# Sliding-window attention with a gated MLP: TensorE transposes the inputs of three batches instead of four, and the hand order of all engines is rewritten

## The chip, the cores and the metric

The kernel runs on one core of one Trainium2 chip, as one launch. The metric is the device time of that launch in microseconds (us), lower is better. Five engines work side by side, each through its own queue in order: TensorE (PE; its weight loads are shown as PEld), VectorE (DVE), ScalarE (ACT), GpSimd (POOL) and SyncE (SP), which here only issues DMA transfers.

## The reference

Causal attention with a window of 64 positions over 8 batches, 8 heads, 576 positions and head size 64; then a gated MLP with a spatial matrix. All inputs and the output are float32.

```python
scores = scale * np.matmul(q, k.transpose(0, 1, 3, 2))        # scale = 1/8
mask = (rel >= 0) & (rel < window)                            # window = 64
attn = softmax(np.where(mask, scores, -1e9))                  # 1e-9 is added to the sum
x = np.matmul(attn, v), heads side by side                    # (8, 576, 512)
h = np.maximum(x @ w_in, 0.0)                                 # 512 -> 1024
u, v = h[..., :512], h[..., 512:]
v_n = (v - mean(v)) / np.sqrt(var(v) + 1e-6)
v_s = np.einsum('ts,bsd->btd', w_spatial, v_n) + b_spatial[None, :, None]
return (u * v_s) @ w_out                                      # (8, 576, 512)
```

## The kernel before, in words

The whole program is one list of words, `ORDER`, that a loop at the end turns into instructions one after the other. There is no scheduler behind it: each word emits its instructions to the engine that it names, so the sequence of words is the sequence of every engine's queue. In a word the first number is the batch b. The second is mostly the pair of heads s (0 to 3, or 4 for the last 64 positions of all pairs) or the block of 128 positions or features j, m or r. A last letter A, D or P says which of ACT, DVE and POOL does a copy.

A batch goes through these steps:

- `l`, `lv`: SP issues the loads of q, k and v in float32. `wl` does it for the eight pieces of w_in; `wsp` and `wout` are issued by POOL.
- `c`, `cv`: casts of q and k, and of v, to float16 (L331 to L346). `sh` (L349 to L360) makes a second copy of v whose keys are shifted by 64 positions. `wc` (L254) casts a piece of w_in on the chip.
- q and k must have the head dimension on the partitions. There are two ways, chosen by `NPE` (L147). For b < NPE the words `T` (L378, L381) are TensorE transposes into a PSUM tile, four for each word, and `to` (L388, L391) copies that tile to SBUF on ACT or DVE: ten `T` and ten `to` a batch, with casts by pair of heads. From batch NPE on the word `R` (L369) is one VectorE transpose of 32x32 blocks of half of q or of k: four a batch, each of [128, 576] 32-bit words, with casts of half of q or k (1152 columns, L337). The loads of q and k differ too: ten a batch (eight of 256 KB and two of 128 KB) in the first way, sixteen of 144 KB, one for each head, in the second; v takes nine and five loads.
- `S`: the scores of two heads. In the first way (L410) 16 matmuls that contract over 64 rows; in the second (L421) 32 that contract over 32 rows, two of them accumulating into each output. `S.b.4` is the last block of queries for all pairs.
- `E` (L453, L460) exponentiates on ACT, `M` (L469) masks on DVE by a minimum with a table, `P` (L486, L496) multiplies by ones (for the sum) and by v on TensorE.
- `n1`, `n2` (L502, L509): logarithm and exp(-log) of the sum on ACT; `x` (L517): the product on DVE, which is x in float16.
- `V` and `Q` (L531, L543): the second half of x @ w_in, block of positions by block; `Q.b` also does the last block of the output of batch b-1 in the other half of the array. `vo` copies with a maximum, `bs` (L562) takes mean and variance, `rs` and `ln` (L580) normalise.
- `U` (L589, L594): the first half of x @ w_in, transposed; `ru` copies it. `G` (L612): the spatial matrix; `g` (L619): the product with `ru`. `O` (L626): the product with w_out; `oc` (L633) copies and `st` stores.
- `W` and `wo` transpose w_spatial once, in the first batch. `H.n` are n matmuls on zeros, at the start only.

Scores and the tile that `P` writes (for s < 4) share a ring of two PSUM tiles ("att", two banks each); all else that TensorE writes goes through a ring of four tiles of one bank ("mm"). A `P` or `S` therefore also waits until the tile two places before it in the ring has been read: a score tile by `E`, a tile of `P` by `x`.

The matmuls use the array in different shapes (rows by columns): 128x128 for `T`, `V`, `U`, `G`, `O`, `W` and `H`; 64x128 for `T.b.x.4`; 128x64 for `P` and `Q`; 64x64 for `S` in the first way; 32x64 for `S` in the second. The transposed scores of one `S` in the first way are written like this:

```python
for h in (0, 1):
    d = slice(64 * h, 64 * h + 64)
    nc.tensor.matmul(sc[r:r + 64, h, o0:o0 + c1 - c0],
                     K[d, p, 64 * key:64 * key + 64], Q[d, p, c0:c1],
                     start=True, stop=True)
```

Of the kernel before, what the change touches and what calls it, by code (L numbers as in the profile page):

```python
# [14 lines left out]
S = 576  # L15
# [17 lines left out]
V.0.0.3.4 vo.0.2.D l.1.q.2 wc.0.0.A V.0.1.0.1 l.1.k.2 bs.0.3 V.0.1.1.2 vo.0.0.A V.0.1.2.3 l.1.k.3
V.0.1.3.4 wc.0.2.A wc.0.1.P T.1.q.0 lv.1.2 vo.0.1.A Q.0 to.1.q.0.D c.1.k.0.P U.0.0 l.1.q.3 vo.0.4.A
cv.1.0.D U.0.4 bs.0.2 ru.0.0 T.1.k.0 U.0.3 sh.1.0.1.D to.1.k.0.A bs.0.4 c.1.q.1.P ones.0 S.1.0
ru.0.4 sh.1.0.0.D U.0.2 E.1.0 bs.0.0 l.1.k.4 U.0.1 bs.0.1 ru.0.3 ru.0.2 T.1.q.1 M.1.0 T.1.k.1 ru.0.1
W.1 to.1.q.1.D rs.0 lv.1.5 W.0 wo.1.A ln.0.4 P.1.0 ln.0.2 to.1.k.1.A c.1.q.2.P W.4 wo.0.D n1.1.0
lv.1.4 ln.0.1 S.1.1 W.2 ln.0.3 n2.1.0 ln.0.0 l.1.q.4 T.1.q.2 wo.4.A W.3 wo.2.D c.1.k.3.P E.1.1
wo.3.D G.0.1 lv.1.6 wout x.1.0 lv.1.7 ones.1 to.1.q.2.D c.1.k.2.P G.0.4 l.2.k.0 M.1.1 T.1.k.2 G.0.2
c.1.k.4.A g.0.1 lv.2.1 cv.1.1.A g.0.4 l.2.q.0 T.1.k.3 sh.1.1.0.P g.0.2 G.0.0 cv.1.2.A to.1.k.2.A  # L40
sh.1.1.1.P c.1.q.4.D c.1.q.3.A sh.1.2.1.P S.1.2 to.1.k.3.D P.1.1 lv.2.0 E.1.2 sh.1.2.0.D T.1.q.4
T.1.k.4 g.0.0 G.0.3 to.1.q.4.A n1.1.1 M.1.2 n2.1.1 lv.1.8 T.1.q.3 g.0.3 P.1.2 l.2.k.1 to.1.k.4.D
n1.1.2 O.0.2 x.1.1 l.2.q.1 n2.1.2 to.1.q.3.D O.0.0 cv.1.3.P l.2.k.2 oc.0.2.A x.1.2 sh.1.3.0.A S.1.3
c.2.k.0.D S.1.4 lv.2.5 E.1.3 O.0.3 oc.0.0.D sh.1.3.1.D lv.2.3 O.0.1 E.1.4 c.2.q.0.D oc.0.3.A M.1.3
l.2.q.4 T.2.q.0 T.2.k.0 oc.0.1.D to.2.q.0.A P.1.3 cv.1.4.D n1.1.3 V.1.1.0.2 M.1.4 sh.1.4.0.P lv.2.2
V.1.3.0.2 n2.1.3 to.2.k.0.D V.1.3.2.3 l.2.q.3 P.1.4 x.1.3 S.2.0 c.2.q.1.P n1.1.4 l.2.q.2 cv.2.0.D
V.1.1.2.3 n2.1.4 V.1.1.3.4 st.0.2 V.1.3.3.4 x.1.4 vo.1.1.A U.1.1 sh.2.0.0.P lv.2.8 vo.1.3.D E.2.0
c.2.k.1.P lv.2.6 bs.1.1 V.1.2.0.2 sh.2.0.1.P l.2.k.3 V.1.0.0.2 c.2.k.2.A M.2.0 T.2.k.1 ru.1.1
V.1.0.2.3 V.1.2.2.3 to.2.k.1.D V.1.2.3.4 lv.2.7 T.2.q.1 cv.2.1.P vo.1.2.A V.1.0.3.4 bs.1.3 st.0.1
P.2.0 vo.1.0.A sh.2.1.1.P Q.1 to.2.q.1.D n1.2.0 l.2.k.4 c.2.q.4.A bs.1.0 c.2.q.2.P S.2.1 vo.1.4.A  # L50
lv.2.4 T.2.k.2 sh.2.1.0.P bs.1.2 T.2.q.2 oc.0.4.A U.1.4 c.2.q.3.P to.2.q.2.A to.2.k.2.D U.1.2 ru.1.4
lv.3.0 n2.2.0 bs.1.4 U.1.3 E.2.1 lv.3.3 x.2.0 c.2.k.3.P U.1.0 rs.1 l.3.q.3 M.2.1 ru.1.2 l.3.k.2
T.2.q.4 ln.1.0 S.2.2 ru.1.3 st.0.0 ln.1.2 P.2.1 ru.1.0 to.2.q.4.D l.3.q.0 ln.1.4 T.2.q.3 n1.2.1
ln.1.1 lv.3.1 T.2.k.3 ln.1.3 G.1.0 E.2.2 to.2.q.3.D l.3.k.0 cv.2.3.A lv.3.6 G.1.1 M.2.2 n2.2.1
sh.2.3.1.P st.0.3 to.2.k.3.D cv.2.4.A G.1.3 x.2.1 cv.2.2.P l.3.q.1 sh.2.3.0.A c.2.k.4.D sh.2.2.1.A
sh.2.2.0.D S.2.3 g.1.0 lv.3.5 T.2.k.4 E.2.3 P.2.2 g.1.3 G.1.2 lv.3.2 n1.2.2 g.1.1 lv.3.4 n2.2.2
M.2.3 G.1.4 to.2.k.4.A l.3.q.2 x.2.2 P.2.3 g.1.2 l.3.k.3 n1.2.3 S.2.4 O.1.1 g.1.4 E.2.4 l.3.k.4
c.3.k.2.D n2.2.3 sh.2.4.0.D O.1.2 l.3.k.1 M.2.4 c.3.q.0.A x.2.3 V.2.2.0.4 oc.1.1.A oc.1.2.A T.3.q.0
c.3.k.0.A vo.2.2.D O.1.0 cv.3.1.P to.3.q.0.A bs.2.2 c.3.q.3.P cv.3.2.A P.2.4 T.3.k.0 n1.2.4 oc.1.0.D
V.2.1.0.4 sh.3.2.1.P n2.2.4 c.3.q.1.A st.1.0 x.2.4 V.2.0.0.4 vo.2.1.D sh.3.1.1.A cv.3.0.P l.4.q.1  # L60
lv.4.1 to.3.k.0.D O.1.3 sh.3.1.0.A c.3.k.1.P st.0.4 bs.2.1 vo.2.0.A sh.3.0.0.P V.2.3.0.4 l.3.q.4
oc.1.3.A bs.2.0 l.4.k.3 sh.3.0.1.P T.3.k.2 vo.2.3.A T.3.k.1 c.3.q.2.P T.3.q.1 l.4.k.4 to.3.k.1.A
S.3.0 to.3.q.1.D c.3.k.3.P l.4.q.3 Q.2 E.3.0 to.3.k.2.D sh.3.2.0.P l.4.q.0 l.4.q.2 S.3.1 vo.2.4.A
M.3.0 T.3.q.2 cv.4.1.P U.2.2 E.3.1 to.3.q.2.D lv.4.0 bs.2.4 T.3.k.3 oc.1.4.A c.3.q.4.P P.3.0 l.4.k.2
ru.2.2 to.3.k.3.D c.3.k.4.P S.3.2 n1.3.0 T.3.q.3 M.3.1 U.2.0 E.3.2 lv.3.8 bs.2.3 U.2.1 st.1.4 n2.3.0
M.3.2 to.3.q.3.A lv.4.3 U.2.3 x.3.0 ru.2.0 rs.2 T.3.q.4 T.3.k.4 ru.2.3 ln.2.2 P.3.2 ln.2.0 ru.2.1
P.3.1 ln.2.1 lv.4.2 to.3.q.4.A ln.2.4 n1.3.2 U.2.4 ln.2.3 G.2.3 n1.3.1 lv.3.7 n2.3.1 cv.3.4.D st.1.3
G.2.1 to.3.k.4.D ru.2.4 sh.3.4.0.P x.3.1 n2.3.2 l.4.q.5 cv.4.0.P st.1.2 x.3.2 G.2.0 st.1.1
sh.4.0.1.P g.2.1 l.4.k.1 S.3.4 g.2.0 l.4.q.7 S.3.3 c.4.q.0.P G.2.2 E.3.3 l.4.k.0 g.2.3 l.4.q.6
cv.3.3.P cv.4.2.A G.2.4 l.4.q.4 g.2.2 sh.3.3.1.P cv.4.3.A O.2.1 g.2.4 E.3.4 l.4.k.6 sh.3.3.0.P M.3.3  # L70
O.2.0 l.4.k.5 sh.4.1.0.P M.3.4 l.4.k.7 oc.2.1.A P.3.3 n1.3.3 O.2.2 l.5.q.1 sh.4.0.0.P R.4.q.0 n2.3.3
O.2.3 oc.2.2.A x.3.3 oc.2.0.A lv.5.2 V.3.0.0.4 c.4.k.0.D l.5.q.2 V.3.3.0.4 R.4.k.0 vo.3.0.A
c.4.q.1.P l.5.k.0 oc.2.3.D P.3.4 l.5.k.3 S.4.0 bs.3.0 n1.3.4 sh.4.1.1.P S.4.1 E.4.0 vo.3.3.D
V.3.2.0.4 lv.5.0 c.4.k.1.P R.4.q.1 n2.3.4 V.3.1.0.4 x.3.4 M.4.0 lv.5.4 U.3.0 vo.3.1.A R.4.k.1 E.4.1
Q.3 bs.3.3 vo.3.2.A P.4.0 lv.5.3 ru.3.0 bs.3.2 lv.4.4 S.4.2 oc.2.4.A bs.3.1 vo.3.4.A U.3.1 n1.4.0
bs.3.4 U.3.2 cv.5.0.P lv.5.1 n2.4.0 M.4.1 l.5.q.7 rs.3 U.3.3 l.5.q.0 E.4.2 x.4.0 U.3.4 l.5.q.3
ln.3.4 ru.3.1 ln.3.1 P.4.1 l.5.k.1 ln.3.0 n1.4.1 S.4.3 ln.3.3 l.5.k.2 ln.3.2 ru.3.2 G.3.1 st.2.2
M.4.2 n2.4.1 st.2.1 E.4.3 x.4.1 G.3.0 ru.3.4 M.4.3 ru.3.3 P.4.2 cv.5.1.A g.3.0 P.4.3 cv.5.4.D n1.4.3
G.3.2 cv.4.4.D n1.4.2 sh.5.4.0.D sh.4.4.0.P lv.6.4 g.3.1 n2.4.2 G.3.3 st.2.0 sh.5.0.1.P g.3.2 n2.4.3
st.2.3 sh.5.0.0.A G.3.4 l.6.k.1 g.3.3 c.5.q.0.P l.5.k.7 O.3.1 x.4.3 l.5.k.4 c.5.k.0.P x.4.2 O.3.2  # L80
# [36 lines left out]
def kernel(  # L117
# [29 lines left out]
    NPE = 4  # L147
# [21 lines left out]
    G = {}  # L169
# [516 lines left out]
```

## Time and profile before

| what | value |
|---|---|
| four runs | 215.09, 213.60, 213.25, 213.35 us |
| their median | 213.48 us |
| the profiled execution's own time | 215.09 us |
| its span, first to last instruction | 213.4 us |
| TensorE, VectorE, ScalarE, GpSimd busy | 201.3, 172.2, 163.6, 64.6 us |
| moved by DMA | 41.47 MB, mean 194 GB/s |
| first matmul, last matmul's start | 1.26 us, about 209.2 us |

The profiled execution is the slowest of the four by its own time, while its span of 213.4 us is close to the times of the other three. The profile lists for each engine the busy time, then the span in 40 slices, the groups of instructions by source line with their mean time, and, on asking, every instruction in order of time. A matmul's shown duration is longer than the time until the next one can start, because matmuls are pipelined; what a group costs TensorE is read from the start of one group to the start of the next. Idle time is shown in square brackets before an instruction, with what ended it.

### The profile page before, as it was taken

What the parts mean: (1) busy time and instruction counts of PE and PEld (TensorE: products, weight loads), DVE (VectorE), ACT (ScalarE), POOL (GpSimd) and SP (SyncE); (2) the same over time, 40 slices, a digit from 0 to 9 for tenths busy, and PEclk for the clock granted to TensorE, in tenths of its full rate; (3) what the DMA queues carried; (4) which work ended last, traced back from release to release, by engine and by line L of the source; (5) the groups of instructions that cost most, each with busy time, mean ns of one, the idle gap of its engine ahead of it and who ended that gap; (6) DMA issues with size and microseconds to landing.
All of it is one profiled execution on the core that took longest, in us unless ns stands there. A gap on an engine that the chain in (4) does not pass through costs nothing.

```text
span 213.4 us, 6682 instructions
## 1 busy us (share of the span) xinstructions
PE 201.3 (94%) x2726; PEld 107.8 (51%) x2726; DVE 172.2 (81%) x359; ACT 163.6 (77%) x305; POOL 64.6 (30%) x93
## 2 busy tenths in 40 slices
PE   7886799899999999999999999998999999999992
PEld 2444335655555655555556455554655555464450
DVE  2377578889999989876999989979999689969642
ACT  3589679978899899967699887974998798564521
POOL 3113641340660327249610804044621600000000
PEclk9999769999999999999999999999999999999998
DMA  5999899899999919999999799999969750102305
GB/s 191 288 237 251 274 214 262 148 250 227 245 228 321 238 47 244 203 223 250 197 180 229 222 231 189 292 231 258 225 114 226 115 197 3 49 34 95 123 39 182
DMA packets 77742, 41.47 MB, mean 194 GB/s; under 512 B 44368, under 2 KB 72080, under 8 KB 77712
## 3 DMA queue, kind: packets, MB, share of 16 engines
q1 hardware_dynamic: 76544, 39.86, 80.6%
q0 software_dynamic: 1168, 1.19, 3.6%
q8 instruction: 21, 0.34, 0.8%
q14 instruction: 9, 0.07, 0.2%
HBM read 32.79 MB, written 9.44 MB: 198 GB/s over the span
## 4 chain that ended last, share of the span: by engine, by line
PE 56%; DVE 10%; ACT 10%; SPq 7%; issue 5%; DMA 5%; POOL 5%; POOLq 0%; DVEq 0%
PE ps L612 14%; PE po L626 10%; PE pv L531 9%; PE pu L589 8%; PE sc L421 4%; SPq L317 3%; PE oz L486 3%; DMA wf<-in_moe_w_in_dram 3%; PE oz L496 3%; DVE st L562 3%; PE pv L543 2%; DMA fq<-in_q_dram 2%; SPq L301 2%; ACT e L453 2%; ACT ru L602 2%
## 5 line engine op out<-in xcount | busy, mean ns | idle before, releaser
L612 PE MATMUL ps<-wspT,vn 128*128 128x512 f16 (+1 forms) x256 | 39.0, 286 | 0.5 <-DVE wspT L276 0.5
L453 ACT ACTIVATE e<-sc 128x1024 f16<-128x1024 f32 x32 | 32.6, 1024 | 3.1 <-PE sc L410 2.8
L531 PE MATMUL pv<-win,x 128*128 128x512 f16 x128 | 33.6, 400 | 1.2 <-DVE x L517 1.1
L517 DVE TENSOR_TENSOR x<-oz,zi 128x512 f16<-128x512 f32 (+1 forms) x40 | 24.9, 629 | 9.5 <-ACT zi L509 9.0
L626 PE MATMUL po<-wout,g 128*128 128x512 f16 x128 | 30.8, 380 | 0.0
L589 PE MATMUL pu<-x,win 128*128 128x512 f16 x128 | 30.5, 380 | 0.1
L502 ACT ACTIVATE ln<-oz 128x512 f32<-128x512 f32 (+1 forms) x40 | 21.8, 555 | 10.3 <-PE oz L496 10.2
L562 DVE BATCH_NORM_STATS2 st<-vs 128x6 f32<-128x512 f16 (+1 forms) x40 | 27.0, 674 | 0.5 <-ACT vs L556 0.2
L619 DVE TENSOR_TENSOR g<-ps,ru 128x512 f16<-128x512 f32 (+1 forms) x40 | 24.2, 628 | 3.6 <-PE ps L612 2.4
L469 DVE TENSOR_TENSOR e<-e,mask 128x1024 f16<-128x1024 f16 x32 | 22.1, 692 | 3.2 <-ACT e L453 3.0
L556 ACT ACTIVATE vs<-pv 128x512 f16<-128x512 f32 (+1 forms) x32 | 18.6, 597 | 7.8 <-PE pv L531 6.5
L612 PEld LDWEIGHTS <-vn 128*128 128x128 f16 x256 | 17.0, 97 | 14.9 <-DVE vn L580 1.8
L509 ACT ACTIVATE zi<-ln 128x512 f32<-128x512 f32 (+1 forms) x40 | 23.3, 590 | 0.6
L602 ACT ACTIVATE ru<-pu 128x512 f32<-128x512 f32 (+1 forms) x40 | 21.1, 558 | 2.5 <-PE pu L594 2.0
L360 POOL COPY vs<-vn 64x512 f16<-64x512 f16 (+1 forms) x15 | 13.0, 872 | 25.1 <-ACT vn L343 10.7
L531 PEld LDWEIGHTS <-x 128*128 128x128 f16 x128 | 11.9, 101 | 15.3 <-issue 2.2
L633 ACT COPY ob<-po 128x512 f32<-128x512 f32 (+1 forms) x21 | 12.1, 587 | 8.7 <-PE po L626 6.5
L589 PEld LDWEIGHTS <-win 128*128 128x128 f16 x128 | 11.8, 98 | 13.1 <-issue 0.6
L626 PEld LDWEIGHTS <-g 128*128 128x128 f16 x128 | 11.5, 98 | 12.3 <-DVE g L619 0.9
L612 PE MATMUL ps<-wspT,vlast 65*128 65x512 f16 (+1 forms) x64 | 17.1, 288 | 0.0
L496 PEld LDWEIGHTS <-vn 128*64 128x64 f16 x320 | 13.8, 113 | 3.8 <-issue 0.4
L496 PE MATMUL oz<-e,vn 128*64 128x64 f16 x320 | 14.1, 197 | 0.0
(133 smaller groups left out, 352.3 us busy)
## 6 DMA issues: line engine op xcount, KB each, us to landing
out_dram<-ob SPq DMA_DIRECT2D x32, 256.0 KB, 3.0
vf<-in_v_dram SPq DMA_DIRECT2D x40, 128.0 KB, 5.8
fq<-in_q_dram SPq DMA_DIRECT2D x32, 144.0 KB, 4.8
fk<-in_k_dram SPq DMA_DIRECT2D x32, 144.0 KB, 4.7
fq<-in_q_dram SPq DMA_DIRECT2D x16, 256.0 KB, 5.4
fk<-in_k_dram SPq DMA_DIRECT2D x16, 256.0 KB, 5.2
vf<-in_v_dram SPq DMA_DIRECT2D x16, 256.0 KB, 6.1
wf<-in_moe_w_in_dram SPq DMA_DIRECT2D x8, 256.0 KB, 6.4
```

Source lines behind the costliest of these rows:

```text
L453: nc.scalar.activation(e2[:, :, :], sc[0][:, :, :], AF.Exp, bias=0.0, scale=0.125)
L469: nc.vector.tensor_tensor(e2[:, :, :], e2[:, :, :], m, ALU.min)
L496: nc.tensor.matmul(oz[64 * h:64 * h + 64, 0, c0:c0 + 64], vt, e2[:, h, c0:c0 + 64], start=True, stop=True)
L509: nc.scalar.activation(zinv[:, 0:n], lnz[:, 0:n], AF.Exp, bias=0.0, scale=-1.0)
L517: nc.vector.tensor_tensor(x[:, 0:n], oz[:, 0, 0:n], zinv[:, 0:n], ALU.mult)
L531: nc.tensor.matmul(PV[b, j][0:jn, :], xcol(b, r, j), w_in_sb[:, r, 512:1024], start=(r == 0), stop=(r == 3))
L562: nc.vector.bn_stats(st6[0:jn, 0:6], VSB[b, j][0:jn, :])
L589: nc.tensor.matmul(pu[:, :], w_in_sb[:, r, 128 * m:128 * m + 128], X[b, r][:, :], start=(r == 0), stop=(r == 3))
L602: nc.scalar.activation(RU[b, m][:, 0:n], pu[:, 0:n], AF.Relu)
L612: nc.tensor.matmul(o, VN[b, kk][0:kn, 128 * mm_:128 * mm_ + 128], w, start=(kk == 0), stop=(kk == 4))
L619: nc.vector.tensor_tensor(g[:, :], ps[:, 0:n], RU.pop((b, m))[:, 0:n], ALU.mult)
L626: nc.tensor.matmul(po[:, :], G[b, r][:, 128 * j:128 * j + 128], w_out_sb[:, r, :], start=(r == 0), stop=(r == 3))
```

## The change

`NPE` goes from 4 to 3, so batch 3 takes the second way (VectorE transposes, scores over 32 rows, loads by head). And the whole of `ORDER` is written anew: the same work for the other batches, in another sequence. In it two `S` of a batch mostly stand next to each other in TensorE's order, and so do two `P`. The letters behind the copies (which engine does them) are chosen anew as well. The number of `H` matmuls stays 29, at other places. w_in is loaded and cast on the chip in both.

```diff
-    NPE = 4
+    NPE = 3
```

TensorE's words from the start to the first `G`, before and after:

```diff
-H.2 H.3 H.3 H.4 H.2 T.0.q.0 T.0.q.1 H.2 T.0.k.0 T.0.k.1 H.3 S.0.0 S.0.1 T.0.k.3 T.0.q.2 H.6 P.0.0
-T.0.k.2 P.0.1 H.4 T.0.q.3 S.0.2 T.0.q.4 T.0.k.4 S.0.3 S.0.4 V.0.3.0.1 V.0.3.1.2 P.0.2 V.0.0.0.1
-V.0.0.1.2 V.0.2.0.1 V.0.2.1.2 P.0.3 P.0.4 V.0.2.2.3 V.0.0.2.3 V.0.3.2.3 V.0.3.3.4 V.0.2.3.4 V.0.0.3.4
-V.0.1.0.1 V.0.1.1.2 V.0.1.2.3 V.0.1.3.4 T.1.q.0 Q.0 U.0.0 U.0.4 T.1.k.0 U.0.3 S.1.0 U.0.2 U.0.1
-T.1.q.1 T.1.k.1 W.1 W.0 P.1.0 W.4 S.1.1 W.2 T.1.q.2 W.3 G.0.1
+H.3 H.3 H.6 H.4 T.0.k.0 H.3 H.2 T.0.k.3 T.0.q.0 T.0.q.2 H.2 T.0.k.1 T.0.q.1 S.0.0 S.0.1 T.0.q.3
+T.0.k.2 P.0.0 S.0.2 H.4 P.0.1 H.2 T.0.k.4 S.0.3 T.0.q.4 V.0.0.0.1 V.0.3.0.1 P.0.2 P.0.3 V.0.1.0.1
+V.0.2.0.1 S.0.4 V.0.2.1.2 V.0.0.1.2 V.0.3.1.2 V.0.3.2.3 V.0.0.2.3 V.0.0.3.4 V.0.2.2.3 V.0.1.1.2
+V.0.1.2.3 V.0.3.3.4 V.0.1.3.4 P.0.4 V.0.2.3.4 U.0.2 U.0.0 T.1.k.1 Q.0 U.0.3 T.1.q.0 U.0.4 U.0.1
+T.1.q.1 W.1 T.1.k.0 W.2 W.0 W.4 S.1.0 S.1.1 W.3 T.1.q.2 T.1.q.3 T.1.k.2 G.0.1
```

SP's first 31 loads, before and after:

```diff
-l.0.q.1 l.0.q.0 l.0.k.3 l.0.k.0 l.0.k.1 lv.0.0 lv.0.1 l.0.q.2 lv.0.3 lv.0.4 l.0.k.2 wl.1.1 lv.0.2
-l.0.q.3 wl.1.0 l.0.q.4 lv.0.5 l.0.k.4 lv.1.0 lv.0.7 lv.0.6 lv.0.8 wl.1.3 wl.1.2 l.1.k.1 wl.0.3
-l.1.q.0 wl.0.2 wl.0.0 l.1.k.0 wl.0.1
+l.0.k.3 l.0.k.1 lv.0.2 l.0.k.0 l.0.q.3 l.0.q.0 l.0.q.1 l.0.q.2 lv.0.0 lv.0.1 l.0.k.2 lv.0.3 wl.0.3
+l.1.q.2 wl.1.0 l.0.k.4 lv.0.7 wl.1.3 l.0.q.4 lv.0.8 lv.0.6 lv.0.4 lv.0.5 wl.0.1 lv.1.2 wl.1.2 wl.1.1
+l.1.q.1 wl.0.2 l.1.k.1 wl.0.0
```

POOL's first words, before and after:

```diff
-id keep c.0.q.0.P c.0.q.2.P c.0.k.2.P c.0.k.4.P wc.1.1.P cv.0.3.P wc.1.2.P sh.0.3.0.P wc.1.3.P wsp wc.0.1.P
+keep id c.0.q.0.P c.0.q.3.P c.0.k.3.P wc.0.3.P cv.0.1.P sh.0.1.0.P c.1.q.2.P wc.1.0.P cv.0.4.P cv.0.3.P
+wc.1.2.P wc.1.1.P wsp wc.0.1.P c.1.q.1.P wc.0.0.P
```

TensorE's words of one later stretch (batch 5's attention beside batch 4's MLP), before and after:

```diff
-S.5.0 S.5.1 P.4.4 U.4.0 V.4.0.0.4 V.4.3.0.4 P.5.0 Q.4 P.5.1 U.4.4 U.4.2 U.4.1 O.3.3 U.4.3 G.4.1 S.5.2
-G.4.0 S.5.4 S.5.3 G.4.2 G.4.3 P.5.3 P.5.4 P.5.2 O.4.1
+S.5.1 S.5.0 Q.4 V.4.2.0.4 U.4.2 U.4.0 U.4.1 U.4.3 P.5.0 P.5.1 G.4.0 G.4.2 G.4.1 S.5.2 S.5.3 G.4.3 G.4.4 S.5.4
+P.5.2 O.4.0 P.5.3 P.5.4 O.4.3
```

## The prediction, made before the changed kernel was run

> **What bounds the kernel now.** I read the page's busy times and slices first, then the busy time of each engine by stage, then TensorE's instructions in order of time.
>
> ```profile
> PE 201.3 (94%) x2726; PEld 107.8 (51%) x2726; DVE 172.2 (81%) x359; ACT 163.6 (77%) x305; POOL 64.6 (30%) x93
> PE   7886799899999999999999999998999999999992
> PEclk9999769999999999999999999999999999999998
> DMA  5999899899999919999999799999969750102305
> ```
>
> TensorE is full from the ninth slice on, and its clock is low in slices 5 and 6. The stages say the same; 41.0 us is the start of the first `G`.
>
> ```profile
> core 0: us, PE busy (x) PEld busy (x) DVE busy (x) ACT busy (x) POOL busy (x), PEclk, DMA share, GB/s
> 0.00:20.40 20.40, 15.94 (x187) 8.20 (x188) 11.22 (x32) 13.66 (x23) 4.99 (x15) 1.00 1.02 236
> 20.40:30.60 10.20, 8.35 (x65) 3.67 (x65) 5.55 (x13) 7.85 (x16) 5.56 (x9) 0.67 0.96 258
> 30.60:41.00 10.40, 9.69 (x127) 5.87 (x128) 9.15 (x22) 8.94 (x18) 2.88 (x5) 1.00 0.99 215
> 41.00:209.40 168.40, 167.14 (x2348) 90.07 (x2347) 146.32 (x294) 132.54 (x250) 51.19 (x65) 1.00 0.82 185
> ```
>
> From 41.0 to 209.4 TensorE is busy for 167.1 of 168.4 us: TensorE's own stream sets this stage. Before 41.0 the start is bound by loads, casts and chains through ACT and DVE. Behind 209.4 lie 4.0 us of the last copy and store.
>
> What a group costs TensorE is the distance to the start of the next, here in batch 3 and in batches 3 and 4:
>
> ```profile
> 82.46 0.39 PE L378 MATMUL tp_1q<-id,nq 128*128 128x128 f16 x4
> 82.78 0.42 PE L410 MATMUL sc<-tr 64*64 64x128 f16 x16
> 83.12 0.40 PE L543 MATMUL pv<-win,x 128*64 128x512 f16 x1
> ...
> 84.46 0.40 PE L378 MATMUL tp_2q<-id,nq 128*128 128x128 f16 x4
> 84.69 1.03 PE L589 MATMUL pu<-x,win 128*128 128x512 f16 x4
> ```
>
> ```profile
> 103.86 0.99 PE L421 MATMUL sc<-tr 32*64 32x128 f16 x64
> 104.78 1.90 PE L531 MATMUL pv<-win,x 128*128 128x512 f16 x8
> 106.52 1.03 PE L589 MATMUL pu<-x,win 128*128 128x512 f16 x4
> 107.48 0.40 PE L543 MATMUL pv<-win,x 128*64 128x512 f16 x1
> ...
> 108.93 0.66 PE L421 MATMUL sc<-tr 32*64 32x128 f16 x32
> 109.52 2.76 PE L589 MATMUL pu<-x,win 128*128 128x512 f16 x12
> 112.12 0.63 PE L594 MATMUL pu<-x,win 128*128 128x64 f16 x16
> ```
>
> A `T` followed by the same shape costs 0.23 us (84.46 to 84.69); a `U` 0.867 (109.52 to 112.12 for three), but 0.96 when another shape follows (106.52 to 107.48). The 0.094 us between them is the price of changing the array's shape; `O`, `G` and `V` show the same 0.09. One `S` over 64 rows costs 0.34 with its change. One over 32 rows costs 0.59 alone (108.93 to 109.52), but two in a row cost 0.92 (103.86 to 104.78).
>
> **Part 1: batch 3's transposes and scores.** Out of TensorE go ten `T`: eight at 0.224 and two of the small kind at 0.127 = 2.05 us. In comes the second form of its scores: before 4 x 0.35 + 0.15 = 1.55; after, two pairs at 1.02 (0.431 + 0.59, their medians after 41 us) and one last block at 0.265 = 2.31; +0.76. Net -1.29, all in the full stage, so on the path. Bounds: 0 if the transposes filled waits (they don't: TensorE has 1.3 us idle in 168), -2.05 if the scores cost nothing more.
>
> The Trainium skill, "VectorE: DVE Perf Modes", section "The three transpose paths", puts a 128x128 transpose at 390 ns on TensorE. An estimate by that page would take 40 x 0.39 = 15.6 us off TensorE; the rows show 56 ns of TensorE's time for each, so the page's is a latency, and the sum stands without it.
>
> The other engines: ten `to` leave (five on ACT at 0.58, five on DVE at 0.68); four VectorE transposes enter at 0.766 (L369, 3.06 us of DVE). Over the whole list, counting each word by its row's mean, DVE loses 4.5 us, ACT 2.7, POOL 0.6. With 146.3 and 132.5 busy of 168.4 none becomes the bound, and I cost their rise in any stretch at nothing; if that cover went, each late copy would cost TensorE its own 0.6 us.
>
> SP: ten loads of q and k become sixteen, nine of v five, so two issues more at 0.47 us. The bytes are equal; a 144 KB load lands in 4.8 us against 5.4 for 256 KB, so per byte up to 1.6 times the DMA work: 9 us of DMA could become 15. From below it is 0. The DMA share over 41 to 209 is 0.82 and batch 3's loads stand more than 10 us of other matmuls ahead of their scores. I cost it at 0.
>
> **Part 2: order.** Counting in the two lists, TensorE changes its shape 117 times before and 104 times after, 12 of the 13 after the first `G`. Price 0.094 to 0.25 (a pair of `S` in part 1 saves 0.16 more than the bare change): -1.1 to -3; I take the plain price, -1.2, since the saving inside batch 3 is counted already. Pricing every group of the two lists from the first `G` to the end by its median agrees: 166.1 before, 163.6 after, -2.5.
>
> The real stage took 168.4, so 2.3 us are waits. Pairs add some: the ring "att" has two tiles, so a pair of `S` fills it, and the next pair waits for two `x`. From the end of a pair of `P` to the second `x`: two `n1` and two `n2` at 0.53 to 0.63 start to start, two `x` at 0.6 to 0.68, 0.3 of signals: 3.7 to 4.1 us. The new order leaves 3.6 to 5.2 us of matmuls there in batches 2 to 7. Shortfall 0 to 0.4 a batch, 0 to 2.8 in all; nearest the lower end, since ACT really starts one `n` every 0.53. I take +0.2. Behind such an `S` stand only `E` and the next `P`.
>
> **Part 3: the start.** Casts that a DMA released tell the bytes landed:
>
> ```profile
> 9.83 0.61 POOL L331 CAST nq<-fq 128x512 f16<-128x512 f32 x1 [4.77 <-DMA fq<-in_q_dram]
> 17.73 0.61 POOL L334 CAST nk<-fk 64x512 f16<-64x512 f32 x1 [5.54 <-DMA fk<-in_k_dram]
> 23.38 0.62 POOL L254 CAST win<-wf 128x512 f16<-128x512 f32 x1 [2.99 <-DMA wf<-in_moe_w_in_dram]
> 28.28 0.61 POOL L254 CAST win<-wf 128x512 f16<-128x512 f32 x1 [0.83 <-DMA wf<-in_moe_w_in_dram]
> ```
>
> Those are the 8th, 18th, 24th and 31st load: 1792, 3584, 4608 and 6400 KB. In the new SP order the v of heads 4 and 5 is the 23rd load instead of the 17th (4480 KB: 22.7 us). `P.0.2` needs its cast and shift (0.44 + 0.6), so it ends near 24.2 instead of 21.0; behind it stand `P.0.3`, two `V` and, through `n1`, `n2`, `x` (2.2 us), `S.0.4` near 26.4 instead of 19.3. Then twelve `V` and `P.0.4` take 2.9 us, or 5.5 at half clock, so `U.0.2` starts at 29.6 to 32.0. Before, `U.0.0` starts at 31.53 with 1.2 us more behind it: the start is -0.7 to +1.7 us late here.
>
> But `W` gates both. `wsp` follows `wc.1.2.P` and `wc.1.3.P` before and is issued at 25.3 to 26.2, landing 10.7 us later at 36.9, where `W.1` starts (36.87). After, it stands behind `wc.1.1.P`, whose load is the 27th (5376 KB: 25.5), so it is issued near 26.1 to 27 and lands near 37.6. From `W.1` to the first `G` the new list has 3.4 us: 41.0, as before. Bounds: 40.3 if the load comes earlier, 44 if everything shifts with `P.0.2` (+3.2). I take 41.0, because the later gate covers what is late ahead of it.
>
> The rows: clock 0.67 from 20.4 to 30.6, after a stretch of small, spread matmuls. The Trainium skill, "TensorE: Matmul & The Clock Gate", section "HAM oscillation", speaks against the new order: an idle window of about 3.4 us brings half rate. By that rule the wait at `P.0.2` makes the `V` behind it cold, the 32.0 end above; by the rows alone either end could come, and the gate of `W` covers both.
>
> **Sum.** 41.0 + 163.6 + 2.3 + 0.2 + 4.0 = 211.1 us of span against 213.4. The profiled execution's own time is 215.09; the other three runs lie at 213.25 to 213.60, so the median 213.48 is the span plus 0.1. Predicted: 211.2 us, 1.1% less.
>
> **Rivals.**
> 1. The start slips (slower). `P.0.2` and all behind it move by 3.2, `W` doesn't cover it, and another window of 3.4 us at half clock adds 1.7: 211.2 + 4.9 = 216.1. It ends above 215.6 when the first `G` starts after 45.4. For it: sixteen `H` ahead of the first `T`, loads in an order with k first, a `P.0.2` that blocks the queue. Against: 31 loads are 6400 KB in both, and w_in is complete near 28.3 in both.
> 2. The gain is eaten by waits of pairs: 2.8 us of shortfall plus batch 3 landing late: 213.4 to 214.
> 3. Back to back saves nothing, because the 0.094 is paid inside the groups as well: only part 1 remains, 212.4. Against: 0.92 for two `S`.
> 4. The start gets shorter. At half clock before, ten `V` cost 2 us too much; if they run at full clock and `W`'s load comes early, the first `G` moves to 39: 209.2.
>
> **Chances.** Forecast (210.0 to 212.3) 0.50; rival 4 0.20; rivals 2 and 3 together 0.15; rival 1 0.15. A measurement of this kernel can tell 1% from no change. Faster by over 1% means below 211.35: 0.6 of the forecast and all of rival 4, 0.50. Slower means above 215.6: most of rival 1, 0.13. Within 1%: 0.37. The range 209.2 to 214.8 leaves out half of rival 1 and part of rival 4.
>
> **What would show it.** Right: 96 `T` instead of 128 at L378, TensorE still 99% busy after the first `G`, that stage near 166 us, the first `G` near 41.0, two `S` of 32 rows at 0.92. Part 3 is wrong if the first `G` starts before 40 or after 42.5; part 2 if TensorE's idle time from there exceeds 3 us, with `x` or `E` named before L410 and L421; part 1 if the stage shrinks by less than 1.3. A start that shifts whole would make the prediction wrong most easily.

## The result, and the profile after

The changed kernel took 216.0 us, the median of 40 runs (213.59 to 218.32); the kernel before took 213.18 (61 runs, 211.92 to 215.28). By the medians that is 1.3% slower. The ratio of the comparable runs is 1.0089, 95% interval 1.0069 to 1.0109; runs over 1.5% above their kernel's fastest are left out of every ratio here, twelve of the changed kernel's among them, so a ratio can lie below what the medians say. The forecast was 211.2, with a range up to 214.8.

In every run listed the time is the span plus 1.7 to 1.9 us. The profiled execution of the changed kernel has a span of 212.4 and a time of 214.08; that is 1.9 us below the median, and only profiled executions show stages. The page's lines of busy time, slices, clock and DMA:

```profile
PE 199.2 (94%) x2766; PEld 104.2 (49%) x2766; DVE 174.4 (82%) x353; ACT 160.6 (76%) x301; POOL 65.0 (31%) x89
PE   7758599999999999999999999999999999999992
PEclk9996969999999999999999999999999999999999
DMA  5999999997999989999699999999599434010514
```

TensorE is idler than before in slices 2, 3 and 5 (7, 5 and 5 tenths against 8, 8 and 7), and its clock is low in slices 4 and 6. Busy time by stage; the first `G` starts at 42.12 us:

```profile
core 0: us, PE busy (x) PEld busy (x) DVE busy (x) ACT busy (x) POOL busy (x), PEclk, DMA share, GB/s
0.00:20.40 20.40, 14.41 (x129) 7.02 (x131) 9.44 (x27) 11.14 (x18) 6.49 (x18) 0.93 1.01 228
20.40:30.60 10.20, 7.80 (x107) 3.68 (x104) 8.09 (x14) 7.44 (x13) 7.09 (x11) 0.83 1.01 288
30.60:42.10 11.50, 11.50 (x137) 6.78 (x136) 9.64 (x24) 8.52 (x19) 2.73 (x4) 0.98 1.18 208
42.10:208.20 166.10, 165.52 (x2402) 86.71 (x2399) 147.19 (x290) 132.89 (x252) 48.66 (x57) 1.00 0.84 186
208.20:212.40 4.20, 0.00 (x0) 0.00 (x0) 0.00 (x0) 0.58 (x1) 0.00 (x0) 0.96 0.40 135
```

The full stage is 166.1 us, where before it was 168.4, and the forecast had 166.1. So the gain came in this execution. It was lost ahead of the first `G`. The kernel before, profiled again, has this start:

```profile
0.00:20.40 20.40, 15.38 (x187) 7.97 (x188) 12.00 (x32) 13.85 (x24) 4.56 (x14) 1.00 1.02 228
20.40:30.60 10.20, 7.96 (x91) 4.10 (x91) 7.63 (x18) 8.49 (x17) 6.77 (x10) 1.00 1.09 300
30.60:39.00 8.40, 7.30 (x104) 4.57 (x102) 7.38 (x17) 8.19 (x16) 2.75 (x4) 1.00 1.05 225
39.00:207.10 168.10, 167.01 (x2348) 89.94 (x2347) 146.46 (x294) 132.21 (x250) 51.77 (x65) 1.00 0.82 186
```

Here the first `G` starts at 39.01, two us earlier than in the profile that the prediction was made from, and the clock is 1.00 in all four stages. The span is 210.9. From the first `G` to the start of `Q.8`, TensorE's last word, the two profiles of the kernel before are 0.5 us apart (167.5 and 167.0 us); the changed kernel takes 165.0. What TensorE waited for in the start, from 8 us to the first `G`, in the changed kernel:

```profile
engine line waited for: us in total, times, longest us
PE oz L484 <- DVE e L467: 2.8, 2, 1.7
PE sc L408 <- DVE tr L386: 1.7, 2, 1.2
PE tp_3k L376 <- POOL nk L329: 1.3, 1, 1.3
PE oz L494 <- DVE vs L358: 0.7, 1, 0.7
PE tp_4k L379 <- ACT nk L332: 0.7, 1, 0.7
```

In the order of time: `T.0.k.3` stands ahead of `S.0.0` and waits for the third cast in POOL's row; `S.0.1` waits for a copy on DVE; `P.0.0` waits 1.74 us for the mask's minimum, and `P.0.3` 1.02. Two more of these lines come from `P.0.2`, whose v is cast late, and from the cast of the last k block. DVE around `P.0.0`, and then POOL beside it:

```profile
12.91 0.68 DVE L386 COPY tr<-tp_1q 128x512 f16<-128x512 f16 x1
14.62 1.69 DVE L467 TENSOR_TENSOR e<-e,mask 128x1024 f16<-128x1024 f16 x1 [1.02 <-ACT e L451]
16.23 0.68 DVE L386 COPY tr<-tp_3q 128x512 f16<-128x512 f16 x1
```

```profile
14.59 0.61 POOL L356 COPY vs<-vn 64x512 f16<-64x512 f16 x1
15.15 0.61 POOL L329 CAST nq<-fq 128x512 f16<-128x512 f32 x1
15.71 1.07 POOL L252 CAST win<-wf 128x512 f16<-128x512 f32 x1
```

The minimum starts late because `E.0.0` does, and it then takes 1.69 us, where its group's mean is 0.79. `P.0.0` in the changed kernel, and then in the second profile of before:

```profile
16.36 0.41 PE L484 MATMUL oz<-e,onesK 128*64 128x512 f16 x2 [1.74 <-DVE e L467]
```

```profile
12.94 0.41 PE L483 MATMUL oz<-e,onesK 128*64 128x512 f16 x2 [0.51 <-DVE e L466]
```

`S.0.0` starts at 12.05 (9.35 in the second profile of before), `P.0.0` at 16.36 (12.94), `P.0.2` ends near 25.3 (21.3), `U.0.2` starts at 32.48 (before, `U.0.0` at 29.11).

### The profile page after: what moved, and what is told of

It reads as the page before. It is cut to its first block, busy times and chain, and to the rows that moved or that the text cites. A ratio compares the mean times of both kernels' runs of the same rounds, so it can differ in the third digit from the quotient of the medians.

```text
span 212.4 us, 6767 instructions
## 1 busy us (share of the span) xinstructions
PE 199.2 (94%) x2766; PEld 104.2 (49%) x2766; DVE 174.4 (82%) x353; ACT 160.6 (76%) x301; POOL 65.0 (31%) x89
## 4 chain that ended last, share of the span: by engine, by line
PE 84%; ACT 5%; DVE 4%; DMA 2%; SPq 1%; issue 1%; POOL 1%; ACTq 0%
PE ps L610 19%; PE pv L529 14%; PE pu L587 13%; PE po L624 12%; PE sc L419 5%; PE oz L484 5%; PE oz L494 4%; PE pv L541 4%; DMA fq<-in_q_dram 2%; DVE e L467 2%; PE pu L592 2%; PE sc L408 1%; ACT e L451 1%; PE wps L269 1%; ACT tr L386 1%
## 5 line engine op out<-in xcount | busy, mean ns | idle before, releaser
L529 PE MATMUL pv<-win,x 128*128 128x512 f16 x128 | 32.3, 396 | 0.0
L554 ACT ACTIVATE vs<-pv 128x512 f16<-128x512 f32 (+1 forms) x35 | 20.4, 597 | 10.4 <-PE pv L529 6.9
L467 DVE TENSOR_TENSOR e<-e,mask 128x1024 f16<-128x1024 f16 x32 | 24.9, 787 | 2.6 <-ACT e L451 2.4
L617 DVE TENSOR_TENSOR g<-ps,ru 128x512 f16<-128x512 f32 (+1 forms) x40 | 24.5, 628 | 2.1 <-PE ps L610 1.9
L335 POOL CAST nk<-fk 128x1152 f16<-128x1152 f32 x8 | 10.6, 1323 | 26.5 <-DMA vf<-in_v_dram 12.7
L631 ACT COPY ob<-po 128x512 f32<-128x512 f32 (+1 forms) x20 | 11.3, 586 | 8.6 <-PE po L624 6.4
L358 POOL COPY vs<-vn 64x1024 f16<-64x1024 f16 (+1 forms) x10 | 9.4, 948 | 24.2 <-PE oz L494 13.1
L356 POOL COPY vs<-vn 64x1024 f16<-64x1024 f16 (+1 forms) x12 | 10.5, 874 | 17.6 <-DVE vn L341 8.0
```

Source lines behind the costliest of these rows:

```text
L467: nc.vector.tensor_tensor(e2[:, :, :], e2[:, :, :], m, ALU.min)
L529: nc.tensor.matmul(PV[b, j][0:jn, :], xcol(b, r, j), w_in_sb[:, r, 512:1024], start=(r == 0), stop=(r == 3))
L617: nc.vector.tensor_tensor(g[:, :], ps[:, 0:n], RU.pop((b, m))[:, 0:n], ALU.mult)
```

## Experiments

Each is compared with runs of the kernel before on the same chip (213.04 to 213.53 us); times are medians.

### The kernel before, unchanged

> The kernel before, unchanged, for a second profile and for the spread of its runs. Theory A (the change makes the stage from the first G shorter by 2.5 us and the start longer, by an amount that differs from run to run): 213.2 us, first G between 38.5 and 41, the stage from there 168.4 us to TensorE's end. Theory B (the loss lies behind the first G in most runs, and the two profiles hide it): also 213.2, but the stage from the first G differs from 168.4 by more than 1 us.

Measured: 212.87 us (10 runs; ratio 0.9989, 0.9957 to 1.0021). What its profile gave is shown above. It also is an experiment on the clock, because the words are the same as in the first profile, and what differs is first of all the windows of half clock (stretches of 3.41 us in which the granted clock is 0.50): that one had two, from 20.4 to 23.8 and from 27.2 to 30.6 us, this one none. Setting each word's start in one against the other, TensorE fell 0.8 us behind by the end of the first window and 1.6 more over the second; 0.4 came back, and the first `G` was 2.0 us apart. In the second window TensorE runs a row of `V`, a `T` and then `Q.0`, without a wait. The row in the first profile, and in the second:

```profile
27.08 3.06 PE L531 MATMUL pv<-win,x 128*128 128x512 f16 x7 [1.09 <-DVE x L517]
```

```profile
26.29 1.68 PE L528 MATMUL pv<-win,x 128*128 128x512 f16 x7 [1.09 <-DVE x L514]
```

### The start of one kernel with the rest of the other

```diff
 # start_before_rest_after: words up to G.0.1 from the kernel before
-    NPE = 4
+    NPE = 3
 # all later words in the new sequence; x.1.0 goes right behind G.0.1
 # start_after_rest_before: NPE = 4, the new words up to G.0.1, the later ones as before
```

> All words up to the first G as before, all others in the order of the changed kernel, three batches transposed by TensorE. Theory A: the short stage without the long start, 213.2 - 2.5 = 210.7 us (210.0 to 211.5). Theory B: the loss comes along, 214 to 216.

Measured: 212.47 us (12 runs; ratio 0.9956, 0.9919 to 0.9993): between the two theories, a miss of theory A's range. Its profile has no window of half clock before the last store; the full stage and the end:

```profile
39.00:205.00 166.00, 164.71 (x2383) 85.94 (x2380) 146.74 (x288) 130.50 (x247) 48.16 (x58) 1.00 0.90 188
205.00:209.20 4.20, 0.00 (x0) 0.00 (x0) 0.00 (x0) 0.58 (x1) 0.00 (x0) 1.00 0.40 132
```

The stage is 2.1 us shorter than in the kernel before, the end 0.4 longer; the profiled spans differ by 1.7, the medians by 0.7 only. The profiled execution is the fastest of the twelve runs; another took 214.06 at full clock, and what made it longer isn't shown. This is the fastest of all kernels here, and the only one whose interval lies below 1.

> All words up to the first G as in the changed kernel, all others in the order of before, four batches transposed by TensorE. Theory A: the long start without the gain, 216.0 + 2.5 = 218.5 us (217 to 220). Theory B: close to before, 213 to 214.5.

Measured: 219.89 us (6 runs; ratio 1.0293, 1.024 to 1.0347). The sign is as theory A has it. The size holds more than the start: at the seam `P.1.0` now stands ahead of the first `G`, and waits 2.19 us for its mask:

```profile
45.44 0.64 PE L483 MATMUL oz<-e,onesK 128*64 128x512 f16 x2 [2.19 <-DVE e L466]
```

Together the two say that the loss lies ahead of the first `G`, and the gain behind it; of a gain of about 2 us in the profiled stage the median keeps 0.7.

### Batch 3 alone

```diff
-    NPE = 4
+    NPE = 3
-T.3.q.0 to.3.q.0.A T.3.k.0 to.3.k.0.D T.3.k.2 T.3.k.1 T.3.q.1 ...
+R.3.q.0 R.3.k.0 R.3.q.1 R.3.k.1
```

> The kernel before with batch 3 alone changed: its q and k transposed by VectorE, its scores over 32 rows, its loads by head; the rest of the order as before, with one S and one E moved behind a G. Theory A and the prediction's part 1: TensorE's stream is 1.29 us shorter in the full stage, 213.2 - 1.3 = 211.9 us (211.3 to 212.6). If the transposes were worth nothing, or the loads by head come late, 213 to 214.5.

Measured: 215.85 us (6 runs; ratio 1.0107, 1.005 to 1.0164): a miss. The first `G` starts at 39.07, so the start is that of before; the stage to `Q.8` takes 169.5 us instead of 167.0. Priced by one table (each kind of group with its neighbour's shape at the tenth percentile of its distances in eight of these kernels), TensorE's groups cost 162.2 us against 163.5, 1.3 less, as worked out; but 7.3 us of the stage lie above these prices instead of 3.5, 3.8 more. What TensorE waited for after 60 us:

```profile
PE pu L589 <- DVE x L512: 1.8, 1, 1.8
PE oz L491 <- DVE vs L353: 0.5, 1, 0.5
PE sc L416 <- DVE tr L364: 0.4, 1, 0.4
```

DVE is late with a product `x` (before, that wait was 0.7), with the copy of v and with a transpose. These waits name about half of the 3.8 us; the rest is not broken down. The edit was put into an order that was not made for it: by its price the term holds, but in this order the waits took more than it gave. In the changed kernel, whose order is all new, none of these waits stands in the trace.

### Pairs split again

```diff
 # start_before_rest_after, 14 times in batches 3 to 7, such as
-S.4.1 S.4.0 U.3.4
+S.4.1 U.3.4 S.4.0
```

> The words up to the first G of the kernel before, the rest of the changed one (212.47 us, 165.0 us from the first G to the last Q), with 14 pairs of neighbouring groups split again: in batches 3 to 7 a G, U, O or V is drawn between two S (8 times) or two P (6 times), so TensorE changes its shape 110 times after the first G instead of 82. Theory (a change costs 0.094 us, and a lone S over 32 rows 0.16 more): 28 x 0.094 + 8 x 0.16 = 3.9 us longer, stage 168.9, time 216.0-216.6. Rival (the change of shape is paid inside the groups as well, adjacency is worth nothing): stage 165.0-165.5, time 212.3-213.0.

Measured: 217.65 us (5 runs; ratio 1.0191, 1.0164 to 1.0217), 1.0 above the theory's range; the stage takes 171.9 us. First the pair in the changed kernel, then the split one:

```profile
105.89 0.99 PE L419 MATMUL sc<-tr 32*64 32x128 f16 x64
106.81 0.64 PE L592 MATMUL pu<-x,win 128*128 128x64 f16 x16
107.29 2.75 PE L587 MATMUL pu<-x,win 128*128 128x512 f16 x12
```

```profile
106.85 0.66 PE L415 MATMUL sc<-tr 32*64 32x128 f16 x32
107.44 0.64 PE L588 MATMUL pu<-x,win 128*128 128x64 f16 x16
108.01 0.67 PE L415 MATMUL sc<-tr 32*64 32x128 f16 x32
108.61 1.90 PE L583 MATMUL pu<-x,win 128*128 128x512 f16 x8
```

The three groups take 107.29 - 105.89 = 1.40 us together and 108.61 - 106.85 = 1.76 split: 0.36 for one pair of `S`, close to the 0.35 of the expectation (two changes and 0.16). A split pair of `P` costs 0.20 (`P.3.3` 0.49 to 0.59, `G.2.4` 0.61 to 0.70). So 8 x 0.36 + 6 x 0.20 = 4.1 us are the price of the changes, near the 3.9 worked out. Of the other 2.8 of 6.9 us the trace names 2.1 as waits that the moved groups brought (3.3 us of named waits behind the first `G` against 1.2). Adjacency is worth what the rows said, and the rival is out.

### The changed start with TensorE kept busy

```diff
+    FILL = {("S", 0, 1): 5, ("P", 0, 0): 7, ("S", 0, 2): 2, ("P", 0, 2): 5, ("P", 0, 3): 4}
+    def fill(t, *key):
+        for _ in range(FILL.get(key, 0)):
+            nc.tensor.matmul(t, scratch[:, 0:128], scratch[:, :], start=True, stop=True)
-H.2 T.0.k.3
+H.7 T.0.k.3
```

> The changed kernel with extra matmuls of the scratch tile in five places where TensorE waits in its start (5 in place S.0.1, 7 at P.0.0, 2 at S.0.2, 5 at P.0.2, 4 at P.0.3, each written into the group's own PSUM tile ahead of its first real matmul, and 5 more in the H ahead of T.0.k.3); nothing else is moved. Theory A (half of the loss is the granted clock: the changed start leaves TensorE idle, so some four windows of 3.41 us at half clock follow, against none or one before; the 40 runs of the changed kernel rise by about 1 us a window): the mean granted clock returns to 0.99 or more and the time falls from 216.0 to 213.2-214.2. Rival B (the late chain through ACT, DVE and POOL alone sets the first G; the clock is a symptom): 215.5-216.5, whatever the clock. If the extra matmuls themselves hold up the chain: above 216.5.

Measured: 215.06 us (11 runs; ratio 1.0077, 1.0043 to 1.011). The clock did as theory A said: 0.993 on average instead of 0.969, which is 0.8 windows of half clock a run instead of 3.8. The time fell by 0.9 only, between the two. The extra matmuls held the chain up: in the profile, which has one such window, `P.0.2` starts at 26.23 instead of 23.53, behind five of them at half clock, and the first `G` at 42.5.

### The kernel before with fewer warm-up matmuls

```diff
-H.3 S.0.0 S.0.1 T.0.k.3 T.0.q.2 H.6 P.0.0 T.0.k.2 P.0.1 H.4 T.0.q.3
+S.0.0 S.0.1 T.0.k.3 T.0.q.2 P.0.0 T.0.k.2 P.0.1 T.0.q.3
```

> The kernel before, without the last three of its nine H (H.3 ahead of S.0.0, H.6 ahead of P.0.0, H.4 ahead of T.0.q.3: 13 matmuls of the scratch tile, on which nothing waits); nothing else is changed. Theory A (idle stretches in TensorE's start bring windows of 3.41 us at half clock, about 0.8 us each, as in the changed kernel): the mean granted clock falls from 0.994 to 0.97-0.985 and the time rises from 213.1 to 214.5-216. Rival B (only the chain of waits counts): the chain is the same or freer, 212.5-213.5.

Measured: 213.23 us (10 runs; ratio 1.0007, 0.9976 to 1.0038). The clock fell as theory A said, to 0.973, and the time stayed as rival B said. The stage in which the clock was low:

```profile
14.00:24.20 10.20, 8.84 (x126) 5.08 (x123) 7.33 (x17) 9.29 (x16) 3.94 (x7) 0.50 1.16 237
24.20:39.60 15.40, 13.19 (x170) 7.69 (x170) 13.30 (x30) 14.08 (x27) 6.44 (x10) 1.00 1.10 249
```

Three windows in a row at half clock, ended at 24.2, and the first `G` at 39.62: 0.6 us later than with full clock. There TensorE waits for casts and copies anyway. So a low clock need not cost time; it does where TensorE has work in a row. The run shows the sum of two changes only: the 13 matmuls are gone as well, and what that alone gave isn't shown.

### The changed start mended

```diff
 # after_v_early
-lv.0.3 wl.0.3 ... lv.0.4 ... lv.0.5 ... x.0.1 sh.0.3.0.D cv.0.2.D ... sh.0.2.1.D
+lv.0.3 lv.0.4 lv.0.5 wl.0.3 ... cv.0.2.D sh.0.2.0.A sh.0.2.1.D ... x.0.1 sh.0.3.0.D
 # after_first_chain
-c.0.k.0.D mask ... c.0.q.3.P c.0.q.1.A c.0.k.3.P c.0.q.2.A T.0.k.3 T.0.q.0 ... S.0.0 ... ones.0 E.0.0
+mask ... c.0.k.0.D ... c.0.k.3.P c.0.q.3.P c.0.q.1.A T.0.q.0 to.0.q.0.A S.0.0 c.0.q.2.A T.0.k.3 E.0.0
 # after_mended: both
```

> The changed kernel with the v loads of heads 4 and 5 issued right behind lv.0.3 (18th and 19th load on SP instead of 26th and 27th among them) and the cast and shifts that P.0.2 waits for put ahead of x.0.1 on DVE. P.0.2 then ends near 24.1 us instead of 25.3. Theory A (the start is one chain, and what P.0.2 loses comes through to the first G): first G 0.8-1.2 us earlier at the same clock, 214.8-215.3. Rival B (a later gate, w_in or wsp, sets it): 215.8-216.3; the loads moved back could even make it later.

Measured: 215.05 us (10 runs; ratio 1.0052, 1.0017 to 1.0088). In the profile `P.0.2` ends at 23.7 and the first `G` starts at 39.97, with one window of half clock, from 16.2 to 19.6 us; this execution is the fastest of the ten. (In the list of loads the two moved from the 22nd and 23rd place to the 13th and 14th.)

> The changed kernel with the first head pair's chain drawn forward: mask made before the first cast, T.0.q.0, its copy, S.0.0 and E.0.0 ahead of T.0.k.3 and of two casts, ones.0 behind E.0.1, M.0.0 ahead of a cast. S.0.0 near 10.7 us instead of 12.05, P.0.0 near 14.6 instead of 16.4. Theory A (one chain): first G about 1.5 us earlier at the same clock, and with less idle TensorE fewer windows at half clock: 213.5-214.5. Rival B (v of heads 4 and 5 and w_in, which land no earlier, set it): P.0.2 still ends near 25.3 and the time is 215.7-216.3.

Measured: 214.47 us (10 runs; ratio 0.999, 0.9949 to 1.003). `S.0.0` starts at 9.98 and `P.0.0` at 14.52, but `P.0.2` still ends at 24.9. The minimum ahead of `P.0.0` took 0.69 us here, at 11.94, with nothing running on POOL.

> The changed kernel with both edits of its start together: v of heads 4 and 5 early, and the first head pair's chain drawn forward. Alone they gave 215.05 and 214.47 against 216.0. Theory A (one chain with two late places behind each other, P.0.0 and P.0.2): the gains add, 213.0-213.8, P.0.0 near 14.5 us and P.0.2 ended near 23.3. Rival B (both gains are the same slack, the later gate takes the rest): 214.3-215.0.

Measured: 213.26 us (12 runs; ratio 1.0001, 0.997 to 1.0031). By the medians the gains add, as theory A has it: 0.95 and 1.53 alone, 2.74 together, though `P.0.2` ended at 24.5 and not at 23.3. By the ratios they don't: about 0.8 and 2.1 us alone, 1.9 together. Clear of noise are the first head pair's chain and both together, not the early v alone. With two places mended the changed kernel is as fast as the one before, so the start is still late by about what the full stage gained.

> The same, and the second head pair drawn forward too: P.0.0 ahead of S.0.1, the cast and shifts of P.0.1 ahead of w_in's casts on POOL and of x.0.0 on DVE. P.0.0 near 12.8 us, P.0.1 near 16.5 (16.4 and 20.0 in the changed kernel). Theory A (the start is this chain until the gate of W holds: wsp is issued near 25.7 and took 10.7 us, so W.1 at 36.2 and the first G at 39.9, like the kernel before): 210.8-212.3, below both kernels. Rival B (contention or another late copy keeps the first G above 41): 213 or more.

Measured: 214.53 us (12 runs; ratio 1.0069, 1.0039 to 1.01): a miss. `P.0.0` starts at 12.82, but `P.0.2` again at 23.1: on ACT `n2.0.1` stands behind the shift of v, which waits 1.65 us for v's cast on DVE, and that stands behind a cast that waits 1.40 us for the last block of q. And three windows of half clock from 20.6 to 30.8 cover the `V`.

```diff
 # after_mended_third: that fault taken out
-n1.0.1 ... c.0.k.4.A c.0.q.4.D cv.0.2.D sh.0.2.0.A sh.0.2.1.D n2.0.1 x.0.1
+n1.0.1 n2.0.1 x.0.1 cv.0.2.D sh.0.2.1.D c.0.q.4.D sh.0.2.0.A c.0.k.4.A
 # after_mended_third_filled: the same, with more scratch matmuls ahead of the V
```

> As after_mended_more, with the fault of that order taken out: n2.0.1 ahead of the shift that waits for v on ACT, x.0.1 ahead of the cast of the late q rest on DVE. P.0.2 begins near 21.5 us instead of 23.1. Theory (a window at half clock costs only where TensorE is full, the V and U stretch from P.0.2 on; otherwise the chain decides): if the V run at full clock the first G comes at 39.5-40.3, where the gate of W lies, and the time is 211.0-212.3; if P.0.1 to P.0.3 still leave TensorE idle enough that the V are cold, 212.5-214. Rival (a half window costs nothing anywhere, as in before_fewer_warm): 211.0-212.0 whatever the clock.

Measured: 214.49 us (6 runs; ratio 1.007, 1.005 to 1.009); a miss too: `P.0.2` starts at 23.6 instead of 21.5. The wait has only moved. From 8 us to the first `G` its longest is now the transpose of the last k block, whose cast stands behind that same shift:

```profile
PE tp_4k L375 <- ACT nk L328: 3.0, 1, 3.0
PE oz L480 <- DVE x L511: 1.2, 1, 1.2
```

> The same words with extra matmuls of the scratch tile where TensorE waits just ahead of the V (3 at P.0.0, 6 at P.0.1, 3 at P.0.2, 2 at P.0.3, H.2 ahead of T.0.k.4 made H.5). Theory: no window at half clock is left behind 24 us in most runs, clock 0.985 or more, and the time is 0.8-2 us below the unfilled one and at 210.8-212.0, below both kernels. Rival (a half window costs nothing): the same as the unfilled one within 0.5 us, or later where the extra matmuls hold the chain up.

Measured: 216.0 us (6 runs; ratio 1.013, 1.0092 to 1.0169). The clock rose (0.990 on average; 0.980 unfilled), and the time rose with it by 1.5 us: the extra matmuls stand in the queue ahead of words that were ready. In the profile `P.0.1`, behind six of them, starts at 18.93 instead of 17.14, and what follows from it is late in turn: the transpose of the last k block starts at 24.03 instead of 21.38.

## Why the prediction was wrong, point by point

**Part 1 (batch 3, -1.29).** Right as a price: 1.3 us by the table of distances in the kernel with batch 3 alone. That kernel's stage was 2.5 us longer, though, and no run has the new order with four batches transposed by TensorE; so what part 1 gave in the changed kernel isn't separated from part 2.

**Part 2 (order).** Right. Of the -2.5 us priced for both parts 2.0 to 2.5 came in the profile: 165.0 us from the first `G` to `Q.8` against 167.0 and 167.5, and 166.1 to TensorE's end, as forecast. Two `S` over 32 rows take 0.92 (105.89 to 106.81), as shown before. The waits of pairs stayed small: TensorE's named waits behind the first `G` sum to 0.6 us.

**Other engines.** ACT fell by 3.0 us, near the 2.7 worked out. DVE was to fall by 4.5 and rose by 2.2 (by 0.9 against the second profile of before): the 32 minima of the mask took 787 ns on average instead of 692, 3.0 us in all, which is less than half of what the forecast was off by; the rest isn't broken down. Behind the first `G` TensorE hardly waits (the 0.6 above), so it cost little there; in the start it is a part of the loss. The Trainium skill, "SBUF — State Buffer", section "SBUF: two separate sides", says that DVE with two inputs from SBUF and GpSimd reading SBUF share a pair of ports under an exclusive lock, so that one blocks for the other's whole instruction. The rows agree in direction: 1.69 us beside three POOL instructions, 1.10 beside one (in the second profile of before), 0.69 with POOL idle. That the lock is the cause was not tested.

**Part 3 (the start, first `G` at 41.0 both ways).** This step failed, twice.

First, "`W` gates both". It did not gate the changed kernel. There `wsp` was issued at 25.66 and 26.5 and landed 9.1 to 9.2 us later, near 34.8 and 35.7, but `W.1` started at 38.35, right behind the word ahead of it:

```profile
L269 PE MATMUL wps<-id,wnat x25: 199/218/243, 38.3 to 41.3; 128*128 128x128 f16 x16, 64*128 64x64 f16 x4, 128*64 128x128 f16 x4, 64*64 64x64 f16 x1
L255 POOL DMA_DIRECT2D wnat<-in_moe_w_spatial_dram x1: 886/886/886, 25.7 to 25.7; - x1
L257 POOL DMA_DIRECT2D wnat<-in_moe_w_spatial_dram x1: 562/562/562, 26.5 to 26.5; - x1
DMA to landing us min/median/max: 9.1/9.2/9.2
```

In the kernel before, the load and TensorE's own words arrive together. In its second profile `W.1` started at 34.46, and only its last weight load waited, 0.25 us; in the run with the pairs split, which has the start of before, TensorE waited 1.0 us there:

```profile
34.91 0.55 PEld L268 LDWEIGHTS <-wnat 64*128 64x128 f16 x6 [0.25 <-DMA wnat<-in_moe_w_spatial_dram]
```

```profile
PE wps L265 <- DMA wnat<-in_moe_w_spatial_dram: 1.0, 2, 0.6
```

So the gate lay within 1 us of TensorE's own stream, and could not cover the 3.2 us by which the prediction itself had `P.0.2` late. In the first profile the load landed just as `W.1` started, but no row there shows TensorE waiting for it, which the cover would have needed. Without the cover what is late ahead goes through, which is the mechanism of rival 1. That its 216.1 fits so well is in part luck: its sum stands on the offset put right below, and the first head pair is not in it.

Second, what was costed of the start was `P.0.2` alone. The first head pair was late too, by 3.4 us at `P.0.0`, through words that the prediction did not price: `T.0.k.3` ahead of `S.0.0`, POOL's row of three casts, the mask behind a cast, `ones.0` ahead of `E.0.0`. Mending each place gave 0.95 and 1.53 us by the medians, both 2.74. The sign that the prediction had named, a first `G` after 42.5, was not met in the profile (42.12), which is one of the faster runs.

**The clock.** The prediction left it open and let the cover of `W` decide. The changed kernel's mean clock over its runs is 0.969, 3.8 windows of 3.41 us at half clock a run; before it is 0.994, 0.8 windows. In its runs the span rises by 0.8 us for each window, from 212.2 with one to 215.8 with six; the runs don't tell whether the windows make a run long or a late chain brings the windows. In its profile the window from 27.7 to 31.1 covers a row of `V`:

```profile
27.68 4.23 PE L529 MATMUL pv<-win,x 128*128 128x512 f16 x11
```

These eleven took 4.17 us to the start of `P.0.4` (31.85); at full clock they take 11 x 0.217 = 2.4, and from 30.6 us to the first `G` TensorE was busy all along. So part of the loss is the clock, 1.8 us in this profile, and the length and spread of the runs (213.6 to 218.3) go with it. How much it is in a median run is not settled: filling the waits brought the clock back and only 0.9 us, but held the chain up; three windows in the start of before, with 13 matmuls fewer, left the time as it was; and the mended kernels change chain and clock together. The Trainium skill, "TensorE: Matmul & The Clock Gate", section "What's actually happening", gives free-running windows of 3413 ns, and the granted clock shows 3.41 us and another phase in every profile. It puts half rate behind an idle window; in the changed kernel's start no idle time is longer than 1.74 us, and its two windows of half clock came behind windows in which TensorE was busy 0.35 and 0.53 of the time. Where the rule and these rows differ, the rows decide: windows that were idle in part were enough. What share it takes isn't shown: in the first profile of before a window busy 0.61 of the time (17.0 to 20.4 us) was followed by half clock, in the kernel with both places mended one busy 0.48 (11.1 to 14.5 us) by full clock.

**The sum.** "Median = span plus 0.1" was wrong: each run's time is its span plus about 1.7. The profiled execution before, with 215.09, lay 1.6 us above the median of its four runs, and its two windows of half clock make a start of 41.0 where 39.0 is had without them. Set right, the two errors nearly cancel: a median run of before starts its first `G` near 39.6 (39.0 and the 0.6 by which the median span, 211.5, exceeds 210.9), so the sum would be 39.6 + 166.1 + 4.0 + 1.7 = 211.4. The miss doesn't come from here.

Put together by medians: 2.8 us longer, though the stage is 2.0 shorter than in the second profile of before and the end 0.4 longer (4.2 against 3.8). If the stage is the same in a median run, which no profile shows, its start must be some 2.8 + 2.0 - 0.4 = 4.4 us later. The profiled run, 1.9 us below the median, shows 3.1 of it; the two mended places gave 2.7 back.

## What to carry to other kernels

A saving in a full stage can be priced from the distances between groups to about half a us, and with an order made for it it came; but a rewritten order must be priced in its start word by word too, each queue from its first load, and a "later gate" counts as cover only if a row shows TensorE waiting for it. Before a sum is set against one profiled execution, look at how its time and clock stand to the other runs. An order tuned as a whole doesn't take single edits: batch 3 alone, and the two kernels that mended the start further, lost more to the next wait than they gained.

## What the runs showed that was not expected

- Windows of half clock depend on how TensorE is used in the start, and what one costs depends on where it falls: nothing visible in the time for three windows where TensorE waits anyway (14 to 24 us; 13 matmuls were left out too), 1.6 us for one over a row of `V` (27 to 31 us).
- The same DVE minimum took 0.69, 1.10 or 1.69 us in the starts of these kernels; the longest stood beside POOL's casts.
- Scratch matmuls that "fill" a wait are not free: they stand in TensorE's order, and at half clock they take twice as long; 28 of them in six places brought the clock from 0.969 to 0.993 and the time down by 0.9 us only.
